# Four edits to the order of a three-stage kernel: edges behind evacuations, quarter reloads, another start, a looser table

## The chip, the cores and the metric

The kernel runs on one core of a Trainium2 chip. The metric is the device time of one execution in microseconds (us); the time given for a kernel is the median of several runs.

## What is computed

The inputs are q, k, v (8 batches, 8 heads, 576 positions, 64 wide), phi (32 memories per position) and the weights of two layers. Per batch and head:

```python
a = softmax over the sequence of phi
k_m, v_m = a^T k, a^T v                  # 32 x 64 each
attn = softmax(q k_m^T / 8)              # over the 32 memories
x = attn v_m                             # 4608 tokens x 512 in all
x = (s * relu(x @ w_in1)**2 + b) @ w_out1      # 512 -> 2048 -> 512
out = relu(x @ w_in2)**2 @ w_out2              # 512 -> 2048 -> 512
```

The weights arrive as 64-bit floats. The kernel takes their words apart itself (`narrow`: one scaling on ACT, then three integer operations on DVE, lines 91 to 99).

## The kernel before, in words

**Stage 1, attention and the first layer's inner product (`hidden`, L418).** v_m and w_in1 are multiplied first (`fold`, L403, four folds of 512 columns a batch), so that relu(attn v_m w_in1) comes out of one product. A batch has SB = 32 *half steps*, called slots: each is six matmuls 128x128 by 288 columns into a PSUM tile `hps` (3 buffers), which ACT evacuates with a relu into `r` (L429). Two half steps make an `r` of 128x576 that SP writes to DRAM (`rd`). Beside the half steps of batch b the work for later batches is done: `front` (maximum of phi, exponential, sum `es`), `kvs` (k_m and v_m, three groups of matmuls), `kv_norm` (1/sum on DVE: `rs`; scaling on ACT: `kn`, `vn`), `kv_turn` (transposes), `q_turn`, `scores`, `q_exp`, `q_sum`, `p_turn`. A table written out by hand (`on(slot, ...)`, L555 to L585) says in which slot each of these is issued. `w1_narrow(i)`, i = 0 to 7, makes the quarters of w_in1; fold n needs quarters 2n and 2n+1. Narrowing of w_out1 (`wo1_narrow`) and its combinations (`wo1_combos`) run as generators, one step in every slot or every second.

**Stage 2, times w_out1 (L666 to L710).** Each matrix product is done on quadrants, seven products e = 0 to 6 in place of eight. A block has 512 tokens, nine blocks; a product e is 48 matmuls of 256 columns in two half steps (uh). Four reloaded activations of 1 MB (`quad`, L477) are squared on ACT (L498), subtracted from each other on DVE (L176, `less`) and split in a high part (ACT cast, L494) and a rest (DVE, L495). `Ready.upto` issues these preparations three half steps ahead. The products run in three PSUM banks in the order "a c a c a b a", so product e = 2 adds to the bank of e = 0, after ACT has read it (`yo`, L696). The four quads of the next block are all requested at e = 4 (L704). Beside it w_in2 is narrowed and combined (`win`, one step in every half step).

**Stage 3 (L760 to L811)** is the second layer's inner product, 384 tokens wide; its results go to DRAM (`gd`), and the combined w_out2 (`wod`) is loaded at its end in two chunks a unit: chunk 0 serves e = 0 to 3, chunk 1 e = 4 to 6. **Stage 4 (L824 to L852)** is the last product, 18 blocks of 168 matmuls.

A scheduler orders each engine's instructions by the program's order and its own estimates; ACT, DVE and SP then run theirs in that order.

## Time and profile before

| what | value |
|---|---|
| median of 3 runs | 1479.03 us (1478.01 to 1480.82) |
| the profiled execution | 1484.73 us, its span 1482.9 us, granted clock 0.993 |
| PE busy in the span | 1418.3 us (96%) |
| DVE, ACT, POOL busy | 1055.7 us (71%), 793.8 us (54%), 19.4 us (1%) |
| DMA | 306.53 MB, mean 207 GB/s |

PE is TensorE's matmuls, PEld its weight loads, SPq the DMA issues of SyncE. Busy time of PE counts pipelined matmuls to their modelled ends. The times are from the start of the span.

### The profile page before, as it was taken

What the parts mean: (1) busy time and instruction counts of PE and PEld (TensorE: products, weight loads), DVE (VectorE), ACT (ScalarE), POOL (GpSimd) and SP (SyncE); (2) the same over time, 40 slices, a digit from 0 to 9 for tenths busy, and PEclk for the clock granted to TensorE, in tenths of its full rate; (3) what the DMA queues carried; (4) which work ended last, traced back from release to release, by engine and by line L of the source; (5) the groups of instructions that cost most, each with busy time, mean ns of one, the idle gap of its engine ahead of it and who ended that gap; (6) DMA issues with size and microseconds to landing.
All of it is one profiled execution on the core that took longest, in us unless ns stands there. A gap on an engine that the chain in (4) does not pass through costs nothing.

```text
span 1482.9 us, 29501 instructions
## 1 busy us (share of the span) xinstructions
PE 1418.3 (96%) x12240; PEld 1365.3 (92%) x12240; DVE 1055.7 (71%) x1461; ACT 793.8 (54%) x1371; POOL 19.4 (1%) x16
## 2 busy tenths in 40 slices
PE   3899899989999999999999999999999999999998
PEld 2678788879998999999999999999999999999998
DVE  6787845466787778788846796885665767676665
ACT  2566566677765666676634554463434344444442
POOL 0002200000000000000000000000000000000000
PEclk9999999999999999999999999999999999999999
DMA  9799966544556665656596757656696344443341
GB/s 301 236 302 328 289 204 224 171 164 154 193 191 204 220 213 186 208 164 215 168 405 241 267 202 259 239 202 207 231 343 248 130 143 143 135 137 112 115 143 29
DMA packets 225045, 306.53 MB, mean 207 GB/s; under 512 B 56080, under 2 KB 182032, under 8 KB 216336
## 3 DMA queue, kind: packets, MB, share of 16 engines
q1 hardware_dynamic: 224752, 304.39, 61.1%
q8 instruction: 96, 1.57, 0.4%
q14 instruction: 37, 0.30, 0.1%
q10 hardware_dynamic: 160, 0.26, 0.0%
HBM read 180.88 MB, written 123.73 MB: 205 GB/s over the span
## 4 chain that ended last, share of the span: by engine, by line
PE 55%; DVE 8%; DMA 6%; ACT 3%; issue 2%; SPq 0%; ACTq 0%; DVEq 0%
PE qa L837 14%; PE pa L781 13%; PE qc L837 7%; PE pc L781 6%; PE ya L686 5%; DVE rcast L495 4%; DMA r<-rd 4%; PE qb L837 3%; PE pb L781 3%; PE yc L686 2%; DVE r L176 2%; ACT rcast L494 1%; DMA wt<-in_moe_w_in_dram 1%; DMA w<-wod 1%; PE yb L686 1%
## 5 line engine op out<-in xcount | busy, mean ns | idle before, releaser
L426 PE MATMUL hps<-pt,vp 128*128 128x288 f32 x1536 | 228.5, 303 | 12.1 <-ACT r L429 11.3
L426 PEld LDWEIGHTS hps<-pt,vp 128*128 128x128 f32 x1536 | 210.3, 191 | 29.1 <-ACT r L429 18.6
L837 PE MATMUL qa<-w,gc 128*128 128x256 f32 x1728 | 219.7, 285 | 2.6 <-DMA w<-wod 1.3
L686 PE MATMUL ya<-rcast,w 128*128 128x256 f32 x1728 | 210.2, 282 | 7.7 <-ACT yo L696 7.2
L837 PEld LDWEIGHTS qa<-w,gc 128*128 128x128 f32 x1728 | 213.9, 194 | 3.3 <-DMA w<-wod 1.5
L686 PEld LDWEIGHTS ya<-rcast,w 128*128 128x128 f32 x1728 | 206.3, 188 | 9.9 <-ACT yo L696 9.0
L730 DVE TENSOR_TENSOR gc<-h,gc 128x1024 fp32r<-128x1024 f32 x119 | 145.2, 1224 | 97.0 <-ACT gc L729 97.0
L781 PE MATMUL pa<-xc,w 128*128 128x384 f32 x1152 | 213.2, 337 | 0.8 <-ACT xc L661 0.7
L495 DVE TENSOR_TENSOR rcast<-r,rcast 128x1024 fp32r<-128x1024 f32 x126 | 150.5, 1219 | 74.8 <-ACT rcast L494 74.7
L781 PEld LDWEIGHTS pa<-xc,w 128*128 128x128 f32 x1152 | 201.0, 188 | 2.1 <-ACT xc L661 1.0
L729 ACT CAST gc<-h 128x1024 fp32r<-128x1024 f32 x119 | 124.5, 1048 | 123.0 <-DVE h L176 108.6
L494 ACT CAST rcast<-r 128x1024 fp32r<-128x1024 f32 x126 | 127.7, 1048 | 35.3 <-DVE r L176 33.3
L429 ACT ACTIVATE r<-hps 128x288 f32<-128x288 f32 x256 | 102.6, 418 | 45.7 <-PE hps L426 38.3
L498 ACT ACTIVATE r<-r 128x2048 f32<-128x2048 f32 x36 | 69.1, 1919 | 77.7 <-DMA r<-rd 77.7
L837 PE MATMUL qc<-w,gc 128*128 128x256 f32 x864 | 110.0, 283 | 0.0
L781 PE MATMUL pc<-xc,w 128*128 128x384 f32 x576 | 108.4, 337 | 0.4 <-DVE xc L662 0.4
L686 PE MATMUL yc<-rcast,w 128*128 128x256 f32 x864 | 106.2, 281 | 2.6 <-DVE rcast L495 1.9
L686 PEld LDWEIGHTS yc<-rcast,w 128*128 128x128 f32 x864 | 103.7, 188 | 3.5 <-DVE rcast L495 2.5
L837 PEld LDWEIGHTS qc<-w,gc 128*128 128x128 f32 x864 | 106.6, 192 | 0.0
L781 PEld LDWEIGHTS pc<-xc,w 128*128 128x128 f32 x576 | 100.7, 188 | 0.8 <-DVE xc L662 0.7
L176 DVE TENSOR_TENSOR r<-r,r 128x2048 f32<-128x2048 f32 x36 | 82.3, 2287 | 0.7
L793 ACT ACTIVATE gr<-pa 128x384 f32<-128x384 f32 x48 | 23.6, 492 | 107.9 <-PE pa L781 107.9
(249 smaller groups left out, 1711.4 us busy)
## 6 DMA issues: line engine op xcount, KB each, us to landing
rd<-r SPq DMA_DIRECT2D x128, 288.0 KB, 3.3
gd<-gr SPq DMA_DIRECT2D x96, 384.0 KB, 3.4
h<-gd SPq DMA_DIRECT2D x34, 1024.0 KB, 5.0
r<-rd SPq DMA_DIRECT2D x24, 1024.0 KB, 7.0
wt<-in_moe_w_out_dram SPq DMA_DIRECT2D x16, 1024.0 KB, 6.7
kv<-in_k_dram SPq DMA_DIRECT2D x24, 384.0 KB, 6.3
kv<-in_v_dram SPq DMA_DIRECT2D x24, 384.0 KB, 6.4
q<-in_q_dram SPq DMA_DIRECT2D x72, 128.0 KB, 3.9
```

Source lines behind the costliest of these rows:

```text
L176: less = lambda out, in0, in1: lambda: nc.vector.tensor_tensor(out=out, in0=in0, in1=in1, op=ALU.subtract)
L426: nc.tensor.matmul(hps[:, :HB], lhsT=w[:, wi], rhs=pt[xi][:, hp, t0:t0 + HB], start=(i == 0), stop=(i == 5))
L429: nc.scalar.activation(r[:, t0:t0 + HB], hps[:, :HB], AF.Relu)
L494: nc.scalar.copy(c[:, :, 0, :], src)
L495: nc.vector.tensor_tensor(out=c[:, :, 1, :], in0=src, in1=c[:, :, 0, :], op=ALU.subtract)
L498: return sums(b11, b12, b21, b22, cast, lambda t: nc.scalar.activation(t, t, AF.Square))
L686: nc.tensor.matmul(to[:, d * 256:d * 256 + 256], lhsT=w[:, wi, d], rhs=cast1[n, e, uh][:, u, xi], start=(start and uh == 0 and d == 0 and ...
L729: nc.scalar.copy(c[:, :, 0, :], of)
L730: nc.vector.tensor_tensor(out=c[:, :, 1, :], in0=of, in1=c[:, :, 0, :], op=ALU.subtract)
L781: nc.tensor.matmul(to, lhsT=w[:, wi, kk], rhs=xc[:, xi, kk], start=(start and n == 0), stop=(n == 5), skip_group_check=True)
L793: nc.scalar.activation(out_, to, AF.Relu)
L837: nc.tensor.matmul(to, lhsT=casts[n, e][:, u, xi], rhs=w[:, wi].rearrange("p k c -> p (k c)"), start=(start and u == 0 and i == 0), stop=( ...
```

## The change

The edges: `behind()` puts an ordering edge from each instruction of a preparation (narrow, combos, exponentials, kv_norm's scalings, casts, squares, subtractions) to the last evacuation recorded on the same engine: the relu or `yo` on ACT, the `yo` update on DVE (in stage 3 the `gr` results). No semaphore is added; the edges only order an engine's own list. Batch 1's front, kvs, norm and turn move from ahead of the first half step into slots 1 to 6; for batches 0 to 2 the sums of exponentials are made by 24 small matmuls (32x2) in each kvs group (72 a batch) in place of a DVE reduction and 8 such matmuls. The table spaces the steps wider (kvs at 8, 17, 26 and not 8, 16, 24; exponentials two slots behind the scores and not one). The quads of a next block are requested one by one, where the last user of a buffer is done: the first two around product 4's preparation, the others around product 6's. Block 0's first square and first casts are issued 8 and 5 slots before stage 1 ends. The generators that load a weight get one or two idle steps between load and use. At the end of stage 3 chunk 1 of units 4 to 7 is loaded last.

```diff
+    st = {}
+
+    def behind():
+        with ExitStack() as edges:
+            for key in ("act", "dve"):
+                if key in st:
+                    edges.enter_context(tc.issue_after(st[key].ins))
+            return edges.pop_all()
+
...
-        nc.scalar.mul(x.bitcast(F32), hw.bitcast(F32), 2.0 ** -112)
+        with behind():
+            nc.scalar.mul(x.bitcast(F32), hw.bitcast(F32), 2.0 ** -112)
...
-            nc.scalar.copy(w[:, part, 0], of)
-            nc.vector.tensor_tensor(out=w[:, part, 1], in0=of, in1=w[:, part, 0], op=ALU.subtract)
+            with behind():
+                nc.scalar.copy(w[:, part, 0], of)
+                nc.vector.tensor_tensor(out=w[:, part, 1], in0=of, in1=w[:, part, 0], op=ALU.subtract)
...
-        less = lambda out, in0, in1: lambda: nc.vector.tensor_tensor(out=out, in0=in0, in1=in1, op=ALU.subtract)
+        def less(out, in0, in1):
+            def go():
+                with behind():
+                    nc.vector.tensor_tensor(out=out, in0=in0, in1=in1, op=ALU.subtract)
+            return go
...
-        if g == NJG - 1:
-            es = at.pop(("es", b))
+        summed = ([at["es", b]] if g == NJG - 1 else []) if b > 2 else [e[:, :, JG * g + j] for j in range(JG)]
+        for i, es in enumerate(summed):
             for n in range(NP):
                 for hp in range(2):
                     r = slice(64 * hp, 64 * hp + 64)
                     nc.tensor.matmul(acc[hp][M * n:M * n + M, 2 * D:2 * D + 2], lhsT=es[r, n], rhs=ones[r],
-                                     start=False, stop=True, tile_position=(64 * hp, M * n), skip_group_check=True)
+                                     start=False, stop=(g == NJG - 1 and i == len(summed) - 1),
+                                     tile_position=(64 * hp, M * n), skip_group_check=True)
+        if g == NJG - 1:
...
-        nc.scalar.activation(r[:, t0:t0 + HB], hps[:, :HB], AF.Relu)
+        st["act"] = nc.scalar.activation(r[:, t0:t0 + HB], hps[:, :HB], AF.Relu)
...
-        return sums(b11, b12, b21, b22, cast, lambda t: nc.scalar.activation(t, t, AF.Square))
+        items = sums(b11, b12, b21, b22, cast, square)
+        if n + 1 < NBLK1:
+            for i, hj in zip((15, 14, 11, 10), QUADS[::-1]):
+                items.insert(i, (None, lambda hj=hj: quads.setdefault(n + 1, []).append(quad(n + 1, *hj))))
+        return items
...
+    front_max(0)
+    front_t1(0)
+    front_t2(0)
+    for g in range(NJG):
+        front_exp(0, g)
     w1_narrow(0)
     for g in range(NJG):
         kvs(0, g)
     kv_norm(0)
-    front(1)
     kv_turn(0)
+    q_turn(0, 0)
+    q_turn(0, 1)
+    scores(0, 0)
+    q_exp(0, 0)
+    scores(0, 1)
+    q_exp(0, 1)
+    q_turn(0, 2)
+    q_sum(0, 0)
+    q_sum(0, 1)
+    w1_narrow(1)
+    p_turn(0, 0)
+    scores(0, 2)
+    q_exp(0, 2)
+    p_turn(0, 1)
+    fold(0, 0)
+    q_sum(0, 2)
+    p_turn(0, 2)
+    front_max(1)
+    front_t1(1)
+    w1_narrow(2)
+    front_t2(1)
     for g in range(NJG):
-        q_turn(0, g)
-    w1_narrow(1)
-    fold(0, 0)
-    for g in range(NJG):
-        scores(0, g)
-        q_exp(0, g)
-        q_sum(0, g)
-    for g in range(NJG):
-        p_turn(0, g)
-    for g in range(NJG):
-        kvs(1, g)
-    kv_norm(1)
-    w1_narrow(2)
+        front_exp(1, g)
     w1_narrow(3)
-    kv_turn(1)
...
+    for g, a in enumerate((1, 2, 3)):
+        on(a, kvs, 1, g)
+    on(4, kv_norm, 1)
+    on(6, kv_turn, 1)
...
-            on(back + 6, front_sum, b)
...
-        for g, a in enumerate((9, 17, 25)):
-            on(z + a, q_exp, b, g)
-            on(z + a + 1, q_sum, b, g)
...
+    for h, hj in ((2, QUADS[0]), (3, QUADS[1]), (20, QUADS[2])):
+        on(SB * (B - 1) + h, lambda hj: quads.setdefault(0, []).append(quad(0, *hj)), hj)
...
-        if slot == SB:
+        if slot == SB + 4:
...
-        if b == B - 1 and h in (4, 16):
-            quads[0] = quads.get(0, ()) + (quad(0, *QUADS[h // 16]),)
-        if b == B - 1 and h == 26:
-            quads[0] += (quad(0, *QUADS[2]),)
+        if slot == SB * B - 8:
+            quads[0].append(quad(0, *QUADS[3]))
+            begun = block_ready(0)
+            ready1.items = lambda n: begun if n == 0 else block_ready(n)
+            begun.pop(0)[1]()
+        if slot == SB * B - 5:
+            ready1.upto(0, 0)
...
-    quads[0] += (quad(0, *QUADS[3]),)
-    ready1.upto(0, 0)
...
-                    nc.scalar.activation(outs[key][:, d], to[:, d * 256:d * 256 + 256], AF.Identity,
-                                         scale=s_sb[:, 0:1], bias=wsum[:, 2 * which + d:2 * which + d + 1])
+                    st["act"] = nc.scalar.activation(outs[key][:, d], to[:, d * 256:d * 256 + 256], AF.Identity,
+                                                     scale=s_sb[:, 0:1], bias=wsum[:, 2 * which + d:2 * which + d + 1])
...
-                nc.vector.scalar_tensor_tensor(out=o, in0=to, scalar=s_sb[:, 0:1], in1=o, op0=ALU.mult, op1=ALU.add)
+                st["dve"] = nc.vector.scalar_tensor_tensor(out=o, in0=to, scalar=s_sb[:, 0:1], in1=o,
+                                                           op0=ALU.mult, op1=ALU.add)
...
-            if e == 4 and n + 1 < NBLK1:
-                quads[n + 1] = [quad(n + 1, *hj) for hj in QUADS]
...
-                    load_unit(wod, "out", u, (1,) if u0 == NU - 2 else (0, 1))
+                    load_unit(wod, "out", u, (0, 1) if u0 < 4 else (0,) if u0 == 4 else ())
+    for u in range(4, NU):
+        load_unit(wod, "out", u, (1,))
```

Place 1, PE ahead of the first half step. `kvs` are k_m and v_m, `vps` the fold, `sp` the scores, `pp` the transposed probabilities, `hps` the half steps. Before:

```order
L411 MATMUL vps<-w_0_165,vmT_171 32x512 x4
L308 MATMUL kvs<-kv,ph 32x128 x20
L411 MATMUL vps<-w_0_165,vmT_171 32x512 x4
L308 MATMUL kvs<-kv,ph 32x128 x23
L367 MATMUL sp<-kb_169,qT 64x64 x12
L308 MATMUL kvs<-kv,ph 32x128 x9
L367 MATMUL sp<-kb_169,qT 64x64 x24
L308 MATMUL kvs<-kv,ph 32x128 x6
L317 MATMUL kvs<-ones,es 32x2 x8
L394 MATMUL pp<-ident,x 128x128 x6
L426 MATMUL hps<-pt_496,vp 128x288
L426 MATMUL hps<-pt_497,vp 128x288
```

And now:

```order
L391 MATMUL sp<-kb_169,qT 64x64 x12
L380 MATMUL qps<-ident,q 128x128 x6
L419 MATMUL pp<-ident,x 128x128 x3
L391 MATMUL sp<-kb_169,qT 64x64 x12
L419 MATMUL pp<-ident,x 128x128 x3
L436 MATMUL vps<-w_0_165,vmT_171 32x512 x8
L451 MATMUL hps<-pt_502,vp 128x288
L451 MATMUL hps<-pt_503,vp 128x288
L451 MATMUL hps<-pt_502,vp 128x288 x2
L451 MATMUL hps<-pt_503,vp 128x288
```

The kvs of batch 1 stand no longer between fold and scores of batch 0; they follow about four half steps later, each group with its 24 small matmuls; the first group:

```order
L380 MATMUL qps<-ident,q 128x128 x4
L451 MATMUL hps<-pt_502,vp 128x288
L451 MATMUL hps<-pt_503,vp 128x288
L329 MATMUL kvs<-kv,ph 32x128 x24
L338 MATMUL kvs<-ones,ph 32x2 x24
```

On DVE batch 1's `rs` (which needs all of that kvs) stands ahead of the narrowing of quarter 3.

Place 2, ACT from behind the evacuation of e = 2 to that of e = 6 in a block of stage 2 (`r` with a number: a quad, its square; `rcast`: casts; `wx`, `wc`: w_in2). Before:

```order
L494 CAST rcast<-r_5742 128x4x256
L498 ACTIVATE r_6179<-r_6179 128x2048
L494 CAST rcast<-r_5742 128x4x256
L498 ACTIVATE r_6182<-r_6182 128x2048
L494 CAST rcast<-r_5742 128x4x256 x2
L494 CAST rcast<-r_6179 128x4x256
L498 ACTIVATE r_6184<-r_6184 128x2048
L494 CAST rcast<-r_6179 128x4x256
L498 ACTIVATE r_6186<-r_6186 128x2048
L494 CAST rcast<-r_6179 128x4x256 x2
L91 ACTIVATE wx<-wt 128x1024
L696 ACTIVATE yo<-ya,wsum,s_sb 128x256 x2
```

And now:

```order
L528 ACTIVATE r_5898<-r_5898 128x2048
L528 ACTIVATE r_6210<-r_6210 128x2048
L522 CAST rcast<-r_5898 128x4x256 x2
L133 CAST wc<-wx 128x256
L528 ACTIVATE r_6272<-r_6272 128x2048
L522 CAST rcast<-r_5898 128x4x256 x2
L522 CAST rcast<-r_6210 128x4x256 x2
L133 CAST wc<-ws 128x3x256
L522 CAST rcast<-r_6210 128x4x256 x2
L744 ACTIVATE yo<-ya,wsum,s_sb 128x256 x2
```

Before, all four squares of the next block (6179 to 6186) stood between casts and ahead of the evacuation of e = 6; now two of them do (6210, 6272), behind the square of this block's last quad (5898), and the other two come after it.

Place 3, SP's queue at the end of stage 3 (`w` from `wod`: 2048 is chunk 0, 1536 chunk 1; `gd` results, `h` the next block). Before:

```order
L213 DMA w_12544<-wod_81 128x2048
L213 DMA w_12546<-wod_81 128x1536
L213 DMA w_12548<-wod_82 128x2048
L213 DMA w_12550<-wod_82 128x1536
L213 DMA w_12619<-wod_83 128x2048
L213 DMA w_12621<-wod_84 128x2048
L797 DMA gd_0_111<-gr 384x1x256 x2
L797 DMA gd_1_112<-gr 384x1x256 x2
L213 DMA w_12681<-wod_83 128x1536
L213 DMA w_12683<-wod_84 128x1536
L750 DMA h_12693<-gd_0_101 128x2048
L750 DMA h_12695<-gd_1_102 128x2048
```

And now:

```order
L233 DMA w_12730<-wod_81 128x2048
L233 DMA w_12732<-wod_82 128x2048
L233 DMA w_12801<-wod_83 128x2048
L233 DMA w_12803<-wod_84 128x2048
L844 DMA gd_0_111<-gr 384x1x256 x2
L844 DMA gd_1_112<-gr 384x1x256 x2
L233 DMA w_12863<-wod_81 128x1536
L233 DMA w_12865<-wod_82 128x1536
L233 DMA w_12867<-wod_83 128x1536
L233 DMA w_12869<-wod_84 128x1536
```

Two chunks 1 (of units 4 and 5) stood ahead of the last two chunks 0; all four now stand behind the last results.

## Rows read from the trace of the kernel before

**Rows 1.** Busy time by stretch: length, PE, PEld, DVE, ACT, POOL, PEclk, DMA share, GB/s.
```profile
0.00:52.80 52.80, 22.95 (x439) 15.61 (x439) 32.73 (x52) 15.87 (x33) 1.21 (x8) 0.97 0.97 300
52.80:104.00 51.20, 48.76 (x573) 37.94 (x573) 41.82 (x73) 33.09 (x74) 0.00 (x0) 0.96 0.79 258
104.00:147.20 43.20, 41.00 (x545) 35.55 (x526) 35.28 (x63) 28.91 (x74) 8.65 (x4) 1.00 1.00 320
147.20:193.10 45.90, 41.93 (x526) 36.90 (x520) 39.21 (x64) 26.73 (x66) 9.58 (x4) 0.96 0.82 267
193.10:232.80 39.70, 39.11 (x529) 34.91 (x521) 21.33 (x44) 24.04 (x63) 0.00 (x0) 1.00 0.70 225
...
313.50:356.30 42.80, 38.32 (x363) 33.17 (x355) 24.56 (x60) 28.64 (x70) 0.00 (x0) 0.96 0.48 168
356.30:385.60 29.30, 26.59 (x200) 25.61 (x192) 23.47 (x37) 26.60 (x60) 0.00 (x0) 1.00 0.69 234
385.60:757.20 371.60, 361.76 (x3025) 358.88 (x3026) 289.65 (x282) 237.60 (x273) 0.00 (x0) 1.00 0.62 202
...
1110.20:1136.20 26.00, 23.42 (x170) 22.72 (x169) 13.79 (x15) 9.30 (x13) 0.00 (x0) 0.87 0.84 309
1136.20:1483.00 346.80, 342.84 (x2858) 342.64 (x2856) 237.70 (x236) 141.28 (x187) 0.00 (x0) 1.00 0.38 122
```

**Rows 2.** Who waited for whom on PE: us in total, times, longest.
```profile
PE hps L426 <- ACT r L429: 11.3, 11, 2.7
PE ya L686 <- ACT yo L696: 7.2, 9, 1.7
```

**Rows 3.** Timeline, ACT near the end of stage 1: start, us, what, [idle before].
```profile
330.86 1.91 ACT L498 ACTIVATE r<-r 128x2048 f32<-128x2048 f32 x1 [2.72 <-DMA r<-rd]
332.67 0.99 ACT L429 ACTIVATE r<-hps 128x288 f32<-128x288 f32 x3
```

**Rows 4.** Timeline of the start, SP, ACT and PE.
```profile
13.53 8.12 SPq L261 DMA_DIRECT2D q<-in_q_dram  x6
...
20.10 1.12 ACT L91 ACTIVATE wx<-wt 128x1024 f32<-128x1024 f32 x1 [3.17 <-DMA wt<-in_moe_w_in_dram]
...
52.83 0.61 PE L426 MATMUL hps<-pt,vp 128*128 128x288 f32 x1 [0.41 <-ACT pt L399]
```

**Rows 5.** Costliest groups by form, DVE: busy us, mean ns, idle before.
```profile
L95 DVE SCALAR_TENSOR_TENSOR wx<-wt,wx 128x1024 int32<-128x1024 int32 x32 | 39.8, 1243 | 0.4
...
L93 DVE TENSOR_SCALAR wx<-wx 128x1024 int32<-128x1024 int32 x32 | 22.3, 697 | 21.7 <-ACT wx L91 21.6
...
L297 DVE TENSOR_REDUCE es<-ph 128x128 f32<-128x1152 f32 x8 | 17.9, 2235 | 2.8 <-ACT ph L293 2.7
...
L372 DVE TENSOR_REDUCE m__441<-sp 128x12 f32<-128x384 f32 x1 | 0.6, 558 | 1.0 <-PE sp L367 1.0
```

**Rows 6.** Timeline, PE, the last kvs group and sums of a batch.
```profile
136.44 0.90 PE L308 MATMUL kvs<-kv,ph 64*32 64x128 f32 x47
137.10 0.17 PE L317 MATMUL kvs<-ones,es 64*32 64x2 f32 x2
...
137.35 0.93 PE L426 MATMUL hps<-pt,vp 128*128 128x288 f32 x5
```

**Rows 7.** Timeline, ACT in stage 2's third block.
```profile
464.16 1.92 ACT L498 ACTIVATE r<-r 128x2048 f32<-128x2048 f32 x1 [6.61 <-DMA r<-rd]
```

**Rows 8.** Timeline, PE in the same block.
```profile
474.65 5.83 PE L686 MATMUL yc<-rcast,w 128*128 128x256 f32 x47 [1.94 <-DVE rcast L495]
481.55 4.65 PE L686 MATMUL ya<-rcast,w 128*128 128x256 f32 x37 [1.07 <-ACT yo L696]
```

**Rows 9.** DMA issues: count, KB each, median us to landing.
```profile
r<-rd SPq DMA_DIRECT2D x24, 1024.0 KB, 7.0
```

**Rows 10.** Timeline, PE at the start of stage 4.
```profile
1116.63 0.62 PE L837 MATMUL qa<-w,gc 128*128 128x256 f32 x3 [1.34 <-DMA w<-wod]
...
1118.65 0.80 PE L837 MATMUL qa<-w,gc 128*128 128x256 f32 x2 [1.05 <-ACT o L843]
```

More of the change, by code (lines that the diff above doesn't have):

```diff
@@ L110, in combos @@
                                   (s3, a11, a21, ALU.subtract), (s4, a12, s2, ALU.subtract)):
-            nc.vector.tensor_tensor(out=out, in0=in0, in1=in1, op=op)
+            with behind():
+                nc.vector.tensor_tensor(out=out, in0=in0, in1=in1, op=op)
             yield
@@ L292, in front_exp @@
         e = at["ph", b][:, :, JG * g:JG * g + JG]
-        nc.scalar.activation(e, e, AF.Exp)
+        with behind():
+            nc.scalar.activation(e, e, AF.Exp)
     def front_sum(b):
@@ L332, in kv_norm @@
             both = acc[hp][:, :D].rearrange("p (o d) -> p o d", o=1).to_broadcast([P, 2, D])
-            nc.scalar.mul(kn[:, hp], both, rs[:, hp:hp + 1])
-            nc.scalar.mul(vn[:, hp], acc[hp][:, D:2 * D], rs[:, hp:hp + 1])
+            with behind():
+                nc.scalar.mul(kn[:, hp], both, rs[:, hp:hp + 1])
+                nc.scalar.mul(vn[:, hp], acc[hp][:, D:2 * D], rs[:, hp:hp + 1])
         at["kn", b] = kn, vn
@@ L377, in q_exp @@
         x = at["x", b, g]
-        nc.scalar.activation(x, x, AF.Exp, scale=scale)
+        with behind():
+            nc.scalar.activation(x, x, AF.Exp, scale=scale)
     def q_sum(b, g):
@@ L553, in on @@
         events.setdefault(slot, []).append(lambda: go(*args))
+    for g, a in enumerate((1, 2, 3)):
+        on(a, kvs, 1, g)
+    on(4, kv_norm, 1)
+    on(6, kv_turn, 1)
     for n in range(1, NV):
-        on((6, 14, 22)[n - 1], fold, 0, n)
+        on((7, 15, 23)[n - 1], fold, 0, n)
     for i in range(4, 2 * NV):
-        on((8, 10, 16, 18)[i - 4], w1_narrow, i)
+        on((5, 9, 13, 17)[i - 4], w1_narrow, i)
     for b in range(1, B):
         z = SB * (b - 1)
-        for g, a in enumerate((8, 16, 24)):
+        for g, a in enumerate((8, 17, 26)):
             on(z + a, scores, b, g)
         if b > 1:
-            y = SB * (b - 2) + (8 if b == 2 else 0)
-            for g, a in enumerate((8, 16, 24)):
+            y = z - SB
+            add, norm, turn = ((20, 27, 33), 35, 37) if b == 2 else ((8, 17, 26), 28, 31)
+            for g, a in enumerate(add):
                 on(y + a, kvs, b, g)
-            on(y + 26, kv_norm, b)
-            on(y + 29, kv_turn, b)
-            first, turn, back = (0, 3, 8) if b == 2 else (y - 15, y - 11, y - 3)
+            on(y + norm, kv_norm, b)
+            on(y + turn, kv_turn, b)
+            first, turn, back = (8, 12, 16) if b == 2 else (y - 15, y - 9, y - 1)
             on(first, front_max, b)
```

57 lines of the change are left out of this document (32 added, 25 removed).

## The prediction

> **What bounds the kernel now.** I read the busy time by stretch first [rows 1]. Stages 2, 3 and 4 are nearly all PE: 361.8 of 371.6 us in stage 2. In stage 1 a full batch takes 39.7 us where nothing disturbs it (193.1 to 232.8), but batches 1, 2 and 6 take 43.2, 45.9 and 42.8 us, batch 0 takes 51.2 us, and the first 52.8 us hold 23.0 us of PE. So PE is the bound nearly everywhere, and what a reordering can win is PE's idle time. The list of waits names most of it: PE's half steps wait 11.3 us for ACT's relu, stage 2 waits 7.2 us for ACT's `yo` [rows 2]. The timeline tells why ACT is late. At 330.9 us ACT sat 2.72 us in front of a square whose quad had not landed, and the relus that stood behind it ran only at 332.7 us [rows 3]. ACT is an in-order queue here: one instruction whose data is late delays the evacuation behind it, and PE is out of buffers. This is what the edges and the earlier reloads touch.
>
> **The start.** The first half step begins at 52.83 us [rows 4]. In the new order batch 1's front and kvs are no longer ahead of it. I walk the new chain: the second quarter of w_in1 lands at 20.1 us, ACT needs until 21.2 [rows 4], and q's last issues end at 21.7 us (13.53 + 8.12), so they land near 24 (an estimate). From 21.2 on DVE works through its list, priced by [rows 5]: narrowing of a quarter, 0.70 + 1.24 + 1.2 = 3.2; maximum and subtraction of three score groups, 6 x 0.56 = 3.4; three sums and two normalisations, about 3.5; batch 1's maximum of phi, a reduction like `es`, 2.2; four small subtractions of half a score group's columns, some 0.35 each, 1.4; two thirds of the next narrowing, 1.9; two fold remainders (512 columns, so some 0.7 each), 1.4. Together 17.0, and 1.5 of waits for q: 39.7 us, 13.1 us earlier.
>
> Most of that is given back in batch 0, because the work moves into it. PE was busy 48.8 of its 51.2 us. Added are three kvs groups of batch 1 (47 records took 137.10 - 136.44 = 0.66 us, 0.87 with the drain: 2.6 us), transposes and front (0.8), and the small sum matmuls. 16 records of these took 137.35 - 137.10 = 0.25 us [rows 6], so 48 take 0.7 us; five groups fall into batch 0 and one into batch 1, 4 us, less 0.25 us for the old ones. By the Trainium skill ("TensorE: Matmul & The Clock Gate", section "Wait — 56ns, not 53.3ns?") starts never come closer than about 25 ns however small the matmul: 48 records would be 1.2 us and the six groups 3 us dearer; the trace shows some 16 ns, and I go by the trace. That makes 56 us of PE work: 39.7 + 56 = 95.7 us if nothing idles. But on DVE `rs` of batch 1 stands ahead of quarter 3's narrowing, so DVE idles from its exponentials until kvs is through; DVE also carries five narrowings (16 us) before the last fold. The two reductions that go (2 x 2.2 us inside batch 0) pay for part of it. I add 3.3 us: batch 1 begins at 99, 5 us earlier than 104. Bounds: 8.3 us earlier with no idling, 2 us later if both DVE and the queue (share 0.97, 0.79, 1.00 in these three stretches) are late. **-5.0.**
>
> **Batches 1 to 7.** Idle PE per stretch [rows 1]: 2.2 in batch 1; 4.0 in batch 2, and its clock of 0.96 means 1.8 us at half clock, that is, of 45.9 us 0.04; 0.6 in batch 3 (4 alike); 4.5 in batch 6 and again 1.7 by the clock; 2.7 in batch 7. Together 18 us. What the change takes away: the square of [rows 3] stands now among the last 8 slots, its load is requested 12 to 29 slots ahead; the w_out1 loads get two more steps, kv_norm's scalings stand behind two relus in place of one. PE waits for ACT only when all three `hps` buffers are full, so a relu that is one half step late costs nothing. I take 1.5 in batch 1 (its kvs sums cost it 0.5), 5 in batch 2, 0.5 in 3 to 5, 5 in batch 6, 2 in batch 7. The bounds are 0 and 18. **-14.0.**
>
> **Stage 2.** Idle PE is 371.6 - 361.8 = 9.8 us. In the third block the square waited 6.61 us for its quad [rows 7]; ACT's casts and the evacuation of e = 0 came late, and PE lost 1.94 us on a cast's remainder and 1.07 on the evacuation, both further back in the same block [rows 8]. Cause: all four quads, 4 MB, were asked for at e = 4, and the first is squared at e = 5. Now the first two are asked for when b22 and b12 are done, some 10 and 15 us into a block of 41 us, and are used at 19 and 23 us; the later two have longer still. These places are read from the new order with the durations above. A quad needs 7.0 us to land [rows 9], so none is late. Against it: `win` has 16 steps a unit, so a whole unit is left for the last block, on DVE's 290 of 372 us; I charge 1 us. Bounds 0 and 10.5 (with 0.7 of small gaps). **-8.5.**
>
> **Stages 3 and 4.** In stage 3 the casts and subtractions are what they were; I take the 1 us of its first waits in half, **-0.5.** Stage 4's first block took 26.0 us at a clock of 0.87; a later one takes 346.8 / 2858 x 168 = 20.4 [rows 1]. The 5.6 us are a wait of 1.34 us for the last chunk 0 [rows 10], 1.05 us for an evacuation held up behind, and the half clock that came with the idling (26 x 0.13 = 3.4). Without two chunks 1 ahead of it the last chunk 0 lands some 4 us earlier, as two of 768 KB at 309 GB/s take 5 us. The chunks 1 of units 4 to 7 land later and are needed 12 us after the start: the last is close. **-4.5**, bounds 0 and -5.6.
>
> **Sum.** -5 - 14 - 8.5 - 0.5 - 4.5 = -32.5. A tenth I keep for new waits of the same kind, +3.0: **-29.5 us**. The profiled execution took 1484.73 us, 5.7 above the median of 1479.03, so it would take 1455.2; against the median, **1449.5 us**. 0.2%, or 3 us, is about what can be told from no change.
>
> **Rivals.**
> - *The start is given back in full* (0.17). For it speaks the DMA share near 1 in the first three stretches and DVE's list; against it that DVE has 9 us of 51 idle in batch 0. Then -5 is gone: 1454.5 us.
> - *The waits move and half of them stay* (0.17). The scheduler still puts squares ahead of data on ACT, and DVE is 78% busy in stage 2. Half of 32.5: about 1463 us.
> - *Slower: the edges hold the preparation back* (0.05). An edge puts a cast behind an evacuation that waits for PE, and what stands behind it cannot pass. The place is stage 2, before e = 1 to 6 of each block. Casts are issued three half steps (8.8 us) ahead; the evacuation may eat one half step, leaving 5.9 us; ACT needs 1.9 + 2.1 us and DVE 2.3 + 2.4 for the same half step. If a step of the weights (1.2 us on either) comes in between, it is just late. A late pair cost 1.94 + 1.07 us [rows 8], so 3 us; seven such in the stage eat its gain of 21 us with stage 2 left out, and two in each of nine blocks give 1479 - 21 + 54 = 1512 us. That queues of ACT and DVE are strict first-in first-out is also what the Trainium skill says ("TensorE: Matmul & The Clock Gate", section "Architectural detail: the array is 16× 32×32, not 1× 128×128"); the trace agrees [rows 3].
> - *No effect* (0.04): what was late by DMA stays late by DMA, and the order was not the cause: 1479 us.
>
> **How the numbers follow.** The forecast has 0.57. Its own range is 1436 (all named idling gone, 43 us) to 1460. The range 1432 to 1467 takes in the first two rivals, with 4 us at either end for what has no name here, and leaves out the slower side, no effect and the far end of the second rival: about 0.85 lies in it. Faster by over 0.2%: 0.57 + 0.17 + 0.17 = 0.91; the same 0.04; slower 0.05.
>
> **What would show it.** Right: the first half step near 40 us, batch 1 near 99, stage 2 in 363 us without a clock below 1.00, stage 4's first block near 21.5, and waits of squares for their quads as in [rows 7] gone. Wrong: PE waits for `rcast` spread over all blocks of stage 2, batch 0 as long as 64 us, or ACT again idle in front of a square with relus behind it.

## The result and the profile after

The changed kernel took **1497.88 us** (1494.04 to 1504.38, 4 runs), the kernel before beside it 1479.92: ratio 1.0125, 95% interval 1.0083 to 1.0167. It is slower by 18 us; I had forecast 1449.5. The profiled execution took 1494.04 us with a span of 1492.3, before 1484.73 and 1482.9. The one lies 3.8 us below its median, the other 4.8 above, so the traces differ by 9.3 us where the medians differ by 18.

The changed kernel's busy time by stretch, columns as in [rows 1]: batch 0 (the start ends at 39.50 us), batches 1 to 7, stage 2, stage 3's first pair, stage 4's first block.

```profile
39.50:111.95 72.45, 59.49 (x887) 46.66 (x887) 45.54 (x81) 33.68 (x79) 0.00 (x0) 0.88 0.75 241
111.95:397.50 285.55, 268.40 (x3273) 238.66 (x3269) 186.50 (x354) 182.61 (x461) 17.71 (x8) 0.99 0.69 220
397.50:761.67 364.17, 359.42 (x3025) 358.32 (x3025) 296.69 (x286) 244.08 (x278) 0.00 (x0) 1.00 0.61 199
761.67:829.96 68.29, 62.32 (x339) 60.94 (x338) 40.64 (x69) 30.61 (x57) 0.00 (x0) 0.95 0.80 306
1122.75:1144.94 22.19, 20.88 (x169) 20.30 (x169) 14.23 (x16) 8.12 (x12) 0.00 (x0) 1.00 0.93 333
```

Two stretches of before that [rows 1] lacks: batches 1 to 7 together, and stage 3's first pair.

```profile
104.00:385.65 281.65, 266.71 (x3186) 237.46 (x3167) 184.73 (x357) 185.50 (x463) 18.23 (x8) 0.99 0.68 224
757.19:817.67 60.48, 59.30 (x338) 58.21 (x337) 40.93 (x70) 30.19 (x57) 0.00 (x0) 1.00 0.80 301
```

| stretch, us | before | after | difference | predicted |
|---|---|---|---|---|
| start | 52.8 | 39.5 | -13.3 | -13.1 |
| batch 0 | 51.2 | 72.5 | +21.3 | +8.1 |
| batches 1 to 7 | 281.7 | 285.6 | +3.9 | -14.0 |
| stage 2 | 371.5 | 364.2 | -7.4 | -8.5 |
| stage 3, first pair | 60.5 | 68.3 | +7.8 | -0.5 |
| stage 4, first block | 26.0 | 22.2 | -3.8 | -4.5 |

The differences add up to 8.5; the rest of the 9.3 lies in the following pairs and blocks. PE's waits in the changed kernel, which answer to [rows 2] (who waited for whom: us in total, times, longest):

```profile
PE pp L419 <- DVE x L411: 17.2, 7, 5.1
...
PE hps L451 <- ACT r L454: 4.9, 5, 1.5
PE pa L828 <- DMA w<-wid: 4.8, 1, 4.8
PE kvs L338 <- issue: 4.4, 2, 3.1
PE vps L436 <- DVE kb L371: 3.8, 1, 3.8
```

The wait for the relu went from 11.3 us to 4.9, that of products for ACT's `yo` is gone, and so are the waits of [rows 10]. In their place stand waits for DVE's `x` and `kb`, for w_in2 and, among the small matmuls of kvs, for nothing that the profile names but issue.

**Batch 0.** PE idled 72.45 - 59.49 = 13.0 us in it, and at a granted clock of 0.88 up to 0.12 x 72.45 = 8.7 us went to the lower of its two levels, 1.2 GHz (before 2.4 and 2.0). The lower level follows the stops: the clock was 0.73 from 58.2 to 66.0 us and 0.79 from 80 to 87, behind the two stops shown next, and 1.00 from 66.0 to 74.5 and from 87 on. Two places of its timeline, PE (with the one row of DVE that waited for it) in batch 1's kvs:

```profile
53.28 0.44 PE L338 MATMUL kvs<-ones,ph 64*32 64x2 f32 x35 [1.25 <-issue]
53.60 0.91 PE L329 MATMUL kvs<-kv,ph 64*32 64x128 f32 x47
54.25 0.16 PE L338 MATMUL kvs<-ones,ph 64*32 64x2 f32 x1
54.26 0.27 PE L329 MATMUL kvs<-kv,ph 64*32 64x128 f32 x1
54.28 0.60 PE L338 MATMUL kvs<-ones,ph 64*32 64x2 f32 x43
57.99 0.27 PE L338 MATMUL kvs<-ones,ph 64*32 64x2 f32 x4 [3.11 <-issue]
...
58.24 0.22 DVE L350 TENSOR_SCALAR rs<-kvs 128x1 f32<-128x1 f32 x2 [9.81 <-PE kvs L338]
```

and DVE between the sum over a score group and the product `x` that PE needs:

```profile
75.06 0.55 DVE L408 TENSOR_REDUCE l__948<-x 128x12 f32<-128x384 f32 x1
75.52 1.22 DVE L112 SCALAR_TENSOR_TENSOR w<-wt,wx 128x1024 int32<-128x1024 int32 x1
...
76.73 2.09 DVE L290 TENSOR_REDUCE pm<-ph 128x128 f32<-128x1152 f32 x1
...
78.99 0.56 DVE L411 TENSOR_TENSOR x<-x,l__948 128x384 f32<-128x384 f32 x1
...
79.69 0.45 PE L419 MATMUL pp<-ident,x 128*128 128x128 f32 x1 [5.14 <-DVE x L411]
```

A step of a narrowing and a maximum of phi, 3.3 us, stand inside this chain, and PE waits 5.1 us. In batch 3 DVE waits for phi's load in front of `kb`:

```profile
201.81 2.10 DVE L290 TENSOR_REDUCE pm<-ph 128x128 f32<-128x1152 f32 x1 [3.08 <-DMA ph<-in_phi_dram]
...
204.09 0.58 DVE L371 COPY kb<-kvt 64x128 f32<-64x128 f32 x2
...
204.81 1.63 PE L436 MATMUL vps<-w,vmT 64*32 64x512 f32 x16 [3.78 <-DVE kb L371]
```

### The profile page after: what moved, and what is told of

It is laid out like the page before. It is cut to its first block, busy times and chain, and to the rows that moved or that the text cites. A ratio compares the mean times of both kernels' runs of the same rounds, so it can differ in the third digit from the quotient of the medians.

```text
span 1492.3 us, 30261 instructions
## 1 busy us (share of the span) xinstructions
PE 1428.3 (96%) x12624; PEld 1375.2 (92%) x12624; DVE 1059.0 (71%) x1458; ACT 794.9 (53%) x1371; POOL 18.9 (1%) x16
## 4 chain that ended last, share of the span: by engine, by line
PE 83%; DVE 8%; DMA 5%; ACT 2%; issue 2%; SPq 0%; ACTq 0%; DVEq 0%
PE qa L886 14%; PE pa L828 13%; PE hps L451 11%; PE ya L734 10%; PE qc L886 7%; PE pc L828 6%; PE yc L734 5%; PE qb L886 3%; PE pb L828 3%; PE vps L436 2%; PE yb L734 2%; DMA ph<-in_phi_dram 1%; PE sp L391 1%; DVE rcast L523 1%; PE kvs L329 1%
## 5 line engine op out<-in xcount | busy, mean ns | idle before, releaser
L451 PE MATMUL hps<-pt,vp 128*128 128x288 f32 x1536 | 233.3, 306 | 6.0 <-ACT r L454 4.9
L451 PEld LDWEIGHTS hps<-pt,vp 128*128 128x128 f32 x1536 | 214.1, 194 | 26.8 <-issue 13.1
L195 DVE TENSOR_TENSOR r<-r,r 128x2048 f32<-128x2048 f32 x36 | 82.0, 2286 | 12.8 <-ACT r L528 12.7
L837 DVE SCALAR_TENSOR_TENSOR gr<-gr 128x384 f32<-128x384 f32 x144 | 76.8, 553 | 2.0
```

What stands on the lines that cost most here:

```text
L195: nc.vector.tensor_tensor(out=out, in0=in0, in1=in1, op=ALU.subtract)
L451: nc.tensor.matmul(hps[:, :HB], lhsT=w[:, wi], rhs=pt[xi][:, hp, t0:t0 + HB], start=(i == 0), stop=(i == 5))
L837: st["dve"] = nc.vector.scalar_tensor_tensor(out=out_, in0=out_, scalar=0.0, in1=out_, op0=ALU.max, op1=ALU.mult)
```

## The experiments

Ratios are to the kernel before, run beside each, with 95% intervals. First come single edits of the changed kernel (1.0125).

### One step less for a unit of w_in2 (e_win15)

```diff
         load(t)
         yield
-        yield
         x = yield from narrow(t, None)
```

> The changed kernel with one of the two idle steps between the load of a w_in2 (or w_out2) unit and its narrowing taken out again, so that a unit takes 15 steps and not 16. Theory: 8 units x 16 = 128 steps do not fit into the 112 half steps of stage 2's first eight blocks, the whole last unit is drained at block 8, its result is written to DRAM at 741 us and the reload of w_in2 for stage 3 starts behind it; with 15 steps that write comes a dozen steps earlier, PE's wait for w of 4.8 us at the start of stage 3 and the half clock behind it go, and stage 3's first pair takes 61 us and not 68. The median falls by about 7 us, to 1491. Rival: the late loads come from the new order of the quads in SP's queue or from the edges, then the wait stays and the time is 1498.

Measured: 1494.8 us, ratio 1.0091 (1.0061 to 1.0121). SP at the end of stage 2, in the kernel before:

```profile
695.86 0.65 SPq L149 DMA_DIRECT2D wid<-wc  x1
...
710.31 0.53 SPq L653 DMA_DIRECT2D x<-x1d  x1
...
736.43 1.28 SPq L213 DMA_DIRECT2D w<-wid  x3
```

in the changed one, with the PE row that waited:

```profile
741.22 0.34 SPq L165 DMA_DIRECT2D wid<-wc  x1
741.65 0.40 SPq L233 DMA_DIRECT2D w<-wid  x1
746.11 0.54 SPq L701 DMA_DIRECT2D x<-x1d  x1
...
747.36 6.75 SPq L233 DMA_DIRECT2D w<-wid  x7
...
776.63 2.26 PE L828 MATMUL pa<-xc,w 128*128 128x384 f32 x6 [4.78 <-DMA w<-wid]
```

and stage 3's first pair in e_win15:

```profile
772.22:832.70 60.48, 59.26 (x338) 58.12 (x337) 40.67 (x69) 29.80 (x57) 0.00 (x0) 1.00 0.81 308
```

The theory holds for this place: the last unit's result is written 45 us later than before, `x`, which takes the room of the units' buffers, loads 36 us later and between the chunks, and PE waits; with 15 steps the pair takes 60.5 us again. Stage 2 gave 1.6 us of it back (365.7 us), for a reason that h_win14 shows. The median fell by 3 us and not by 7, and its interval overlaps the changed kernel's.

This run also tells how far one trace can be trusted in stage 1. ACT, DVE and SP run there in the same order as in the changed kernel, and yet batches 1 to 7 took 295.2 us, not 285.6. So differences of a few microseconds between single traces of stage 1, as in the next runs, show nothing by themselves; the medians and the lists of waits carry more.

### Sums of exponentials on DVE (e_es)

```diff
-        summed = ([at["es", b]] if g == NJG - 1 else []) if b > 2 else [e[:, :, JG * g + j] for j in range(JG)]
+        summed = [at["es", b]] if g == NJG - 1 else []
```

> The changed kernel with the sums of exponentials of batches 0, 1 and 2 made by one reduction on DVE again (8 small matmuls at the end of kvs in place of 24 in each group). Theory: in batch 0 the two stalls of PE among the small matmuls (1.25 and 3.11 us, ended by issue, each about when a 16 KB packet of the instruction queue has landed) come from PE running 127 matmuls and as many weight loads of some 17 ns each in 2.2 us, faster than its instructions arrive; with a third of the small ones gone the stalls go, with them most of the half clock from 55.6 to 62.5 us, DVE's wait of 9.8 us for kvs shrinks, and batch 0 takes some 64 us and not 72, the median 1491. Against it stand two reductions of 2.2 us on DVE in the start, which may put the first half step some 2 us later. Rival: PE waited for the k and v data or for ACT, and the stalls stay under another matmul; then batch 0 stays at 70 to 74 us and the time at 1498 to 1500.

Measured: 1489.92 us, 1.0065 (1.0047 to 1.0083). The stalls for issue among the sums are gone but for 0.4 us, and the first half step still begins at 39.5 us; but batch 0 took 69.9 us, not 64, since the wait of 5.1 us for `x` and a clock of 0.88 stayed; batches 1 to 7 gave 1.4 us, which is within the noise. The median came as forecast, the place only in part.

### The maximum of phi behind older DVE work (e_pm)

```diff
+        with ExitStack() as edge:
+            if "work" in at:
+                edge.enter_context(tc.issue_after(at["work"].ins))
```

> The changed kernel with an ordering edge on DVE that puts the maximum of phi behind the last piece of fold, kv_turn or q_sum work issued before it in the program (in the changed kernel it stands 3 to 18 slots ahead of its place, right where its load is about to land). Theory: DVE's waits for the load of phi (9.2 us) and the 2.1 us of the maximum itself in front of kb and of x (L371, L411) are what PE's waits at 79.7, 124.5, 158.1, 204.8 and 247.7 us (5.1, 2.2, 2.3, 3.8, 1.4) rest on; they go in good part, DVE waits for phi no longer, and batches 1 to 4 lose 6 to 9 us, the median falls to 1488 to 1492. Rival: DVE is late by its amount of work and the waits move to the same matmuls behind another instruction: no more than 2 us.

Measured: 1493.36 us, 1.0083 (1.0053 to 1.0113). DVE's waits for phi fell from 9.2 us to 3.8, PE no longer waits for `kb` in batch 3, and batches 1 to 7 took 281.6 us (285.6). PE's waits for `x` stayed (16.7 us), behind narrowing steps and small instructions of 2 us beside POOL. Batch 0 took 83.4 us: its first half step came 4 us earlier, at 35.5, and a stall of 4.8 us for issue is new. The interval overlaps the changed kernel's. Half right: the maximum accounts for the `kb` waits, not for `x`.

### The sum over w_out1 on DVE, not POOL (e_wacc)

```diff
-            nc.gpsimd.tensor_tensor(out=wacc, in0=wacc, in1=wo1[u], op=ALU.add)
+            with behind():
+                nc.vector.tensor_tensor(out=wacc, in0=wacc, in1=wo1[u], op=ALU.add)
```

> The changed kernel with the running sum over w_out1 (wacc) added on DVE in place of POOL, 8 instructions. Theory: a small DVE instruction on 12 columns (L409, 0.17 us) took 2.00, 2.05 and 2.05 us each time POOL's addition ran beside it and ended with it, and a copy 2.42 us; without POOL these four give back 8 us of DVE, and PE's waits for x at 158.1, 177.6 and 235.1 us (2.3, 1.2, 1.5) shrink to some 2 us together; DVE pays 8 x 1.2 = 10 us elsewhere. The median falls by 2 to 4 us. Rival: DVE's own additions hold up the same chains as long, and nothing changes within 1 us.

Measured: 1492.61 us, 1.0086 (1.0052 to 1.0120), an interval that overlaps the changed kernel's. The small instruction took at most 176 ns now, but PE waited 16.0 us for `x` as before (17.2) and batches 1 to 7 took 288.6 us. The contention is real; that it costs this kernel time isn't shown.

### The old start, the old table (c_start, c_table)

```diff
-    for g, a in enumerate((1, 2, 3)):
-        on(a, kvs, 1, g)
-    on(4, kv_norm, 1)
-    on(6, kv_turn, 1)
```

> The changed kernel with the start of before: front, kvs, norm and turn of batch 1 and three quarters of w_in1 ahead of the first half step, sums of exponentials on DVE for all batches; edges, looser table and all the rest as changed. Theory: the 8 us by which batch 1 begins later than before come from the new start, as DVE's and PE's waits and the half clock of batch 0 cost more than the 13 us that the first half step is earlier; with the old start the first half step begins at 53, batch 1 at 104 to 106, and the median falls by 6 to 8 us to 1490 to 1492. Rival: the table's new places in batch 0 (fold, scores, narrowing) or ACT's edges make batch 0 long whatever stands ahead of it; then batch 1 begins at 112 or later, and with the first half step at 53 perhaps at 116.

```diff
-        for g, a in enumerate((8, 17, 26)):
-            on(z + a + 2, q_exp, b, g)
-            on(z + a + 3, q_sum, b, g)
+        for g, a in enumerate((9, 17, 25)):
+            on(z + a, q_exp, b, g)
+            on(z + a + 1, q_sum, b, g)
...
```

> The changed kernel with the table of before for scores, exponentials, sums, turns, folds and kvs from batch 1 on (kvs of batches 3 up, and their front) and the w_out1 loads with one idle step; the new start, edges and everything else as changed. Theory: in the looser table sums stand three and not two half steps behind scores and turns no further back for it, and the load of phi is asked for two half steps later while kb and scores wait behind its maximum; with the old places PE's waits for x and kb in batches 1 to 4 (2.2, 2.3, 1.2, 3.8, 1.5, 1.4) and the half clocks behind two of them go, batches 1 to 7 take 278 us and not 285.5, the median is about 1490. Rival: the waits come from the new start's lateness or from the order that the scheduler chose, not from the places in the table: within 2 us of 1498.

Measured: 1490.2 us, 1.0052 (1.0024 to 1.0079), and 1489.92 us, 1.0076 (1.0051 to 1.0101). With the old start the first half step began at 53.6, batch 1 at 111.4: batch 0 took 57.7 us, not 51, so that batch 1 did not begin earlier, as the rival had it. Whether the new places in batch 0 or the edges cost the difference is not settled: h_newtable below, with the old start, the new scores in batch 0 and no edges in stage 1, takes 53.8. The median fell all the same. With the old table batches 1 to 7 took 281.3 us; the interval of that run overlaps the changed kernel's. Each edit is worth some 8 us by the medians and none is the whole.

### Stages 2 to 4 of the change alone, with and without edges (h_edges2, h_plain)

h_edges2 has stage 1 of the kernel before, and 15 steps a unit. h_plain differs from it in

```diff
-            for key in ("act", "dve"):
+            for key in ():
```

> The kernel before with its whole stage 1 (start, table, sums, no edges there) and of the change only what concerns stages 2 to 4: edges behind evacuations in stages 2 and 3, quads of the next block requested one by one, the order of the w_out2 chunks; w_in2 units keep 15 steps. Theory: the change's gains lie here and its losses elsewhere; stage 2 takes 364 us (before 371.6), stage 3's first pair 60.5, stage 4's first block 22.2 (before 28.2), stage 1 ends at 386 as before: 13 us less, median 1467. Rival: stage 2's gain in the changed kernel came from the preparation that stage 1 had already done for block 0 or from the slower weights, and part of it is lost: 1473 or more.

> The same without any edge (the blocks that would add them add none). Theory: what helped stage 2 is that no square stands in front of an evacuation while its quad has not landed, and this comes from the quarter reloads: without edges stage 2 still takes 364 to 366 us and the median stays within 3 us of the kernel with edges (1467 to 1470). Rival: the edges did it, by keeping casts and squares behind yo; then PE's waits for yo return, 7 us in nine times, and the median is 1474.

Measured: 1469.28 us, **0.9944** (0.9918 to 0.9971), and 1478.08 us, 0.9992 (0.9971 to 1.0014). ACT's wait of squares for their quads in stage 2, of which [rows 7] is one (us, times, longest), in the kernel before,

```profile
ACT r L498 <- DMA r<-rd: 71.9, 30, 6.6
```

in h_plain,

```profile
ACT r L523 <- DMA r<-rd: 70.6, 30, 5.0
```

and in h_edges2:

```profile
ACT r L523 <- DMA r<-rd: 9.7, 5, 3.1
```

Stage 2 took 371.5, 370.9 and 362.3 us, and PE's wait for `yo` was 7.2, 7.8 and 0 us. So the rival on h_plain is right: without edges ACT's order still puts a square where its quad has not landed, and `yo` behind it. The edges win the stage.

The requests one by one do nothing, and the reason is that they do not leave earlier. SP's rows for quads of block 1, in the kernel before (block 0 begins at 385.65 us),

```profile
398.25 5.72 SPq L483 DMA_DIRECT2D r<-rd  x3
...
411.91 4.40 SPq L483 DMA_DIRECT2D r<-rd  x2
```

and in h_plain (383.89 us):

```profile
396.34 5.73 SPq L505 DMA_DIRECT2D r<-rd  x3
...
410.15 5.29 SPq L505 DMA_DIRECT2D r<-rd  x3
```

They leave 12.6 and 26.3 us into block 0 before, 12.5 and 26.3 in h_plain, 12.3 and 27.0 in h_edges2; in the other blocks h_plain's first request leaves within 2 us of the place it had before. In front of such requests SP waited for DVE, 146.5 us in stage 2 before and 148.6 in h_plain, so a request's place in the program did not decide when it left. What the edges changed is when the squares run: later, when their data is there. (Edges with the old place of the requests were not run.)

Stage 4's first block took 22.3 us in h_edges2 and 21.1 in h_plain, counted as for before (26.0); of the change only the order of the chunks bears on it in both.

### Edges in stage 1 (h_edges1, h_block0, e_noedge1)

h_edges1 is h_edges2 with the relu recorded; h_block0 adds the change's requests for block 0; e_noedge1 is the changed kernel without that record.

```diff
-        nc.scalar.activation(r[:, t0:t0 + HB], hps[:, :HB], AF.Relu)
+        st["act"] = nc.scalar.activation(r[:, t0:t0 + HB], hps[:, :HB], AF.Relu)
```

> The kernel of h_edges2 (stage 1 of before, stages 2 to 4 of the change) with the edges in stage 1 too: ACT's exponentials, kv_norm's scalings, narrowings and squares stand behind the last relu issued. Theory: in stage 1 the edges act on ACT alone (DVE has no evacuation recorded there), they take PE's waits for relu from 9.9 to some 4 us with the half clocks behind them and nothing on DVE gets later, so stage 1 ends 4 to 6 us earlier (377 to 379 and not 382.6) and the median is 1464. Rival: an edge that puts an exponential behind a relu makes the sums and x on DVE late, as in the changed kernel, and stage 1 ends at 386 or later: 1472 or more.

> The kernel of h_edges1 with the quads of block 0 requested as in the change (half steps 2, 3 and 20 of the last batch and 8 ahead of its end) and its first square and casts issued there. Theory: the square that waited 2.7 us for its quad at the end of batch 6, with relus behind it and a half clock, is gone: batch 6 takes 36.7 us and not 38.8 to 42, the first products of stage 2 give up to 2 us of that back, as in the changed kernel, whose first block took 43.1 us: the median is 1 to 4 us below that of h_edges1. Rival: edges alone already put that square behind the relus, and block 0 gets longer by as much as batch 6 gets shorter: no difference within 1 us.

> The changed kernel without the edges in stage 1 (no relu is recorded, so nothing is put behind one), all else as changed. Theory: the edges are not what made stage 1 longer; without them PE's waits for relu come back (from 4.9 to 8 or more us) and the time is 1498 to 1503. Rival: the edges hold exponentials back two half steps and so x and kb on DVE; without them PE's waits for x (17.2 us) shrink by half, batch 0 to 4 get 8 to 10 us shorter, the time is 1489.

Measured: 1481.19 us, 1.0006 (0.9990 to 1.0021); 1477.11, 0.9967 (0.9954 to 0.9980); 1499.03, 1.0104 (1.0064 to 1.0144). PE's waits in h_edges1:

```profile
PE pp L416 <- DVE x L408: 5.3, 5, 2.7
...
PE ya L717 <- ACT rcast L517: 5.0, 1, 5.0
PE hps L448 <- ACT r L451: 4.6, 3, 3.2
```

In h_edges2 the relu cost 9.9 us and `x` 2.2. So the edges do halve the waits for relu, and hand them on to `x` (and `kb`, 3.4 us); batches 1 to 7 took 287.2 us, not 277.8. h_best below differs from h_block0 in these edges alone: with them PE's waits in batches 1 to 7 are 3.2 us for relu (8.8) and 8.1 for `x`, `kb` and `pt` (0.5).

In the traces over half of h_edges1's loss against h_edges2 lies where the stages meet. The 5.0 us for `rcast`, which the 287.2 contain, are PE's wait ahead of stage 2's first product. DVE made three of block 0's large subtractions before the last relu in h_edges2 and none of them in h_edges1, as the squares and casts ahead of them stood behind the relus. Stage 2's first block, in h_edges2 and then in h_edges1:

```profile
382.57:422.40 39.83, 39.83 (x336) 39.83 (x337) 27.78 (x29) 24.87 (x28) 0.00 (x0) 1.00 0.58 182
391.50:435.50 44.00, 42.88 (x337) 42.40 (x338) 38.35 (x36) 29.28 (x32) 0.00 (x0) 0.93 0.48 153
```

In the ten traces with these edges this block took 42.7 to 44.0 us, in the eight without 39.8 to 39.9. All of stage 2 took 370.5 us in h_edges1, 367.0 in h_block0 and 362.3 in h_edges2. Block 0's early casts take away the 5.0 us wait, 4 us by the medians, but the three subtractions still come late. So the rival's time came on the old table, and its mechanism is a part of it.

In the changed kernel the edges cost nothing by the medians: without them PE waited 17.4 us for relu and 9.4 for `x`, with them 4.9 and 17.2; batches 1 to 7 took 298.0 us (285.6) and stage 2 359.8 (364.2).

### Each suspect alone on the best base (h_best, h_noexp, h_newstart, h_newtable)

h_best is h_block0 without edges in stage 1. h_noexp is h_block0 with

```diff
-        with behind():
-            nc.scalar.activation(x, x, AF.Exp, scale=scale)
+        nc.scalar.activation(x, x, AF.Exp, scale=scale)
...
```

and h_newstart and h_newtable add the change's start and its table to h_best.

> The kernel of h_block0 without the edges in stage 1: stage 1 of before, block 0's quads and first casts as in the change, edges and quarter reloads in stages 2 to 4. Theory: the edges of stage 1 cost what h_edges1 lost against h_edges2 (12 us), block 0's earlier quads gain what h_block0 won against h_edges1 (4 us); without the first and with the second the median is 1465 to 1468, and stage 2 begins at 381 or earlier. Rival: the gain of block 0's quads hung on the edges (without them the scheduler puts the square ahead of its data again), then it is 1470 or more.

> The kernel of h_block0 with no edge on the exponentials and on kv_norm's scalings; those of narrowings, combinations and squares stay in stage 1. Theory: an exponential behind a relu makes the sums and x late on DVE, as x and kb wait there behind reductions; freed of it, PE's waits for x and kb in batches 1 to 3 (1.7, 2.7, 1.8 us) and the half clocks behind them go, batches 1 to 3 take 130 us and not 134, the median is 1466 to 1470. Rival: it is the narrowing behind the relus that delays DVE's chain; then no more than 2 us below h_block0's 1477.

> The kernel of h_best with the new start alone: batch 1's front, kvs and norm behind the first half step, sums of batches 0 to 2 by small matmuls, batch 0's folds, narrowings and the steps of batch 2 at the change's places; table of before from batch 1 on, no edges in stage 1. Theory: the start is what moved batch 1's begin from 104 to 112; it begins at 110 to 113 here too (first half step at 39 to 40, batch 0 72 us with PE's stalls for instructions and x), and the median is 7 to 10 us above h_best. Rival: with the edges and the looser table gone batch 0 is shorter, batch 1 begins at 104 or earlier and the time is that of h_best or better.

> The kernel of h_best with the looser table alone from batch 1 on (scores, folds, exponentials, sums, turns, kvs of batches 3 up, two more idle steps for w_out1 units). Theory: the wider places bring the maximum of phi, whose load is asked for two half steps later, in front of kb and x on DVE and cost 4 to 8 us in batches 1 to 4: batches 1 to 7 take 281 to 286 us, the median is 4 to 8 us above h_best. Rival: the waits came from the edges on ACT or from the late start; alone the table changes nothing (within 2 us).

Measured, all four on one chip: 1469.94 us, 0.9940 (0.9921 to 0.9959); 1475.66, 0.9964 (0.9948 to 0.9979); 1482.66, 1.0024 (1.0011 to 1.0038); 1486.95, 1.0054 (1.0034 to 1.0074). Batch 0, then batches 1 to 7, in h_best,

```profile
53.10:104.20 51.10, 48.75 (x574) 37.90 (x574) 41.82 (x73) 33.12 (x75) 0.00 (x0) 0.97 0.79 255
104.20:380.10 275.90, 264.60 (x3169) 235.93 (x3164) 185.47 (x357) 183.94 (x463) 18.31 (x8) 0.99 0.69 229
```

batch 0 in h_newstart,

```profile
39.00:111.10 72.10, 60.02 (x896) 45.16 (x896) 47.33 (x84) 35.34 (x82) 0.00 (x0) 0.88 0.74 236
```

and batches 1 to 7 in h_newtable, with four rows of its timeline, one of DVE and three of ACT:

```profile
105.40:396.30 290.90, 271.84 (x3176) 240.10 (x3165) 188.69 (x356) 184.71 (x461) 18.01 (x8) 0.98 0.67 218
...
162.24 3.30 DVE L107 SCALAR_TENSOR_TENSOR wx<-wt,wx 128x1024 int32<-128x1024 int32 x1
...
167.64 0.52 ACT L400 ACTIVATE x<-x 128x384 f32<-128x384 f32 x1 [4.33 <-DVE x L394]
168.07 0.99 ACT L451 ACTIVATE r<-hps 128x288 f32<-128x288 f32 x3
...
342.19 1.91 ACT L525 ACTIVATE r<-r 128x2048 f32<-128x2048 f32 x1 [4.59 <-DMA r<-rd]
```

The start is slower by itself: batch 1 begins at 111.1 with or without edges. The table is too, 15 us in batches 1 to 7, and phi's load, which I expected, is at most a part (DVE waited 3.1 us for it): ACT sits 4.3 us in front of an exponential whose `x` is late, with three relus behind it, and PE's waits for relu rise to 15.4 us (8.8). Ahead of that `x` a narrowing step took 3.30 us, beside POOL's addition, where one takes 1.2. PE's longest wait, 4.1 us, stands behind the last row, a square of block 0 whose quad was late; in h_best that square waited 0.9 us. ACT's waits for `x` add up to 30.0 us in h_newtable and 28.5 in h_best, so which place of the table costs the time is not settled. Taking exponentials out of the edges won no more than 1.5 us over h_block0, within the intervals, so their edges are not the cause there; that the narrowing's are, as the rival has it, is not shown. Block 0's early quads are worth nothing without edges in stage 1 (h_best and h_edges2 are alike).

### 14 steps a unit (h_win14)

```diff
         x = yield from narrow(t, None)
-        yield
         made = {}
```

> The kernel of h_best with 14 steps for a w_in2 (or w_out2) unit, as many as a block of stage 2 has half steps (the idle step behind the narrowing is taken out). Theory: in blocks 6 to 8 of h_best (40.4, 41.6 and 41.8 us against 39.76) the wide pieces of a unit's combination fall on the half steps in which DVE subtracts twice and casts for the next product, since with 15 steps a unit moves on by one half step a block; with 14 every block meets them where block 0 does (39.86), the three blocks take 39.9 each, PE's three waits for rcast of 1.6 us go, and the median is 3 to 4 us below h_best, 1466. Rival: it is the last quads or the loads for stage 3 that make these blocks long; then nothing changes within 1 us.

Measured: **1464.62 us, 0.9896** (0.9862 to 0.9929), the best version found. Block 8 of stage 2 (counted from 0, as in the expectation), in h_best,

```profile
700.76:742.42 41.66, 40.02 (x338) 39.83 (x337) 29.52 (x30) 21.84 (x28) 0.00 (x0) 1.00 0.71 267
```

and in h_win14:

```profile
700.86:740.63 39.77, 39.77 (x338) 39.77 (x337) 24.52 (x21) 18.24 (x21) 0.00 (x0) 1.00 0.68 259
```

Block 8 and block 6 (40.3 to 39.75) came as expected, and PE's three waits for `rcast` (3.6 us) are gone; block 7 (41.6 to 41.2) has a wait of 1.2 us for `yo` left. Stage 2 took 359.4 us, before 371.5 and in h_best 362.3; the intervals of these two versions' ratios just overlap.

## Why the prediction was wrong

- **Start.** "39.7 us" was right: 39.5. "That makes 56 us of PE work" was too high (59.5 busy less up to 8.7 by the clock is 51; it also counts all six groups of small matmuls in batch 0, where five fall, and charges the sixth to batch 1 again), and **"I add 3.3 us" for idling failed**: 13.0 us of idling and a clock of 0.88. I had seen that `rs` holds DVE's narrowing (it sat 9.8 us), and priced DVE by its busy sum. What I didn't price was the order inside its queue (a narrowing step and a maximum inside the chain to `x`), the lower clock behind the stops, and that PE could stop among the small matmuls for issue (4.4 us).
- **Batches 1 to 7, "-14.0".** The relu's waits did fall, in this stretch from 11.3 us to 3.6. The step that failed is that the idling would go, with a tenth kept "for new waits of the same kind": I asked what is late on ACT and not who waits next. DVE has no evacuation recorded in stage 1, so no edge orders it; PE's waits for `x` and `kb` in this stretch rose from 0.5 us to 12.4. The looser table is slower by itself (h_newtable).
- **Stage 2, "-8.5".** It measured -7.4, near the forecast by luck: the cause I gave, that the quads were asked for at e = 4 and "now the first two are asked for" some 10 and 15 us into a block, is wrong. That is where they stood in the program. In the trace of before the first requests left at 12.6 and 17.8 us already, and h_plain, with the new places and no edges, gains nothing. The edges did it, and those in stage 1 took some 3 us of it away again in the first block (43.1 us).
- **Stage 3, "-0.5".** It measured +7.8. I saw the whole unit left for the last block and charged "1 us" of DVE, without following it to its write, `x` and the reload of w_in2.
- **Stage 4, "-4.5".** Right: -3.8.
- **The rivals.** "The edges hold the preparation back" is a mechanism that the runs show (h_edges1), but through the edges of stage 1: they delay `x` and `kb` there and block 0's preparation for stage 2, not each of the nine blocks. It is not what makes the changed kernel slow (e_noedge1). "The start is given back in full" was too mild by 8 us.

From h_best (1469.9) to the changed kernel (1497.9) the single costs by the medians are 12.7 for the start, 17.0 for the table, 7.2 for stage 1's edges (h_block0) and 3.1 for the 16th step, together 40 for 28 measured. The first two are clear of the noise. The intervals behind the last two overlap, and their runs stand beside others of the kernel before; by the ratios they are some 4 and 5 us. The edges and the table share a part, since with the table the edges cost nothing. How the 12 us split is not settled by these runs.

## What to carry to other kernels

On an in-order queue an edge can move the lateness to the next queue; follow each moved step to the engine that needs its result, and price the order there, not the busy sum. (Whether edges on DVE too would have kept the gain was not run.) Look also at where the edges end: work that they hold behind a stage's last evacuation lands in the next stage. A generator's steps have to fit the slots that drive it: with 16 a unit a load moved across a stage's end, and with 14, as many as a block has slots, eight of nine blocks took 39.8 to 39.9 us. Read from the trace, not from the program, when a request leaves: here it left when SP's wait ended, wherever it was written, and what helped was to run its user later.
